# New spans for the parts of all head pairs in a scheduled kernel of attention and mixture-of-experts attention

## The chip, the cores and the metric

The kernel runs on one core of a Trainium2 chip. The metric is the device time of one launch, in microseconds (us). Three runs of the kernel before took 783.99, 787.72 and 788.71 us; the median is 787.72 us.

## The reference

Two layers of causal attention stand one behind the other. The first has 8 batches of 8 heads, 576 positions and 64 columns a head, and a learned decay; the second is a mixture of 4 experts, each an attention with one head of 64 columns over the 512 columns that the first layer gives, of which the two with the highest gate logits count at each position.

```python
# layer 1: q, k, v (8, 8, 576, 64), f (8, 8, 576)
scores = q @ k.T / 8
cum = cumsum(log(clip(f, 1e-4, 1)))
scores = where(causal, -1e9, scores + cum[:, :, :, None] - cum[:, :, None, :])
attn = exp(scores - max(scores)); attn /= sum(attn) + 1e-9
x = (attn @ v).transpose(0, 2, 1, 3).reshape(8, 576, 512)
# layer 2: w_gate (512, 4), wq, wk, wv (4, 512, 64), wo (4, 64, 512)
logits = x @ w_gate            # the two largest are kept, softmax over them is w
for e in range(4):
    q, k, v = x @ wq[e], x @ wk[e], x @ wv[e]
    a = causal_softmax(q @ k.T / 8)
    out += w_e * (a @ v @ wo[e])   # where e is one of the two experts
```

## The kernel before, in words

**Pairs.** The work is cut into 48 pairs of 64-row heads: in each batch four pairs of attention heads (kind "a", names such as a5_1 for batch 5, pair 1) and two pairs of experts (kind "m"). They follow each other in one list: the four "a" pairs of batch b, then the two "m" pairs of batch b-1. Two heads of 64 columns fill the 128 rows of TensorE (PE).

**Parts of a pair.** Every pair goes through the same parts, each a generator that emits its instructions in pieces.
- *prep*: an "a" pair transposes k and q (tp, L269), a "m" pair projects x by wk and wq (pp, L406, 12 matmuls to a half). Values are split into a high part, copied by ScalarE (ACT, L277 or L413), and the rest, subtracted by VectorE (DVE, L278 or L414). SyncE's DMAs move copies across partitions into the tiles kq and ka (L246).
- *vals* loads v. *front*, once per batch of experts, projects v and the gates (pv, L330; pg, L377), the gates on DVE.
- *max*: matmuls m0 to m3 (L432), masked maxima of them on DVE (L438, L449, L482), a transpose of the maxima (mp, L487), a negating copy on ACT (ms, L489), and a DMA (L246) that puts the negated maxima into one row of kq.
- *scores*: s0 (two), s1, s2 (two), s3 (two) in PSUM, each accumulated from a first half (L518), which needs prep alone, and a second half (L519), which also needs the row of negated maxima. ACT takes the exponential (L538 for s0, L548 for s1, L553 for s2, L565 and L569 for s3) into the tiles P and pl, GpSimd (POOL) clears what lies above the diagonal (L540, L504, L570) and adds up the parts (L576 to L579) into R.
- *attend*: P times v (oa and ob, L600, 4 and 10 matmuls), copied out to ot by ACT (L618, L626).
- For two pairs together, *sums*: column sums (sm, L643), their reciprocals on DVE (zt, L655 to L668) and a copy on ACT (rt, L669); then *apply*: for each of the two pairs two matmuls that spread the reciprocals over rows (cp, L686), two products on DVE (L687), a high part on ACT (L704) and a rest on DVE (L705), which form the input x of the experts (xh, xl) or of the output (yh, yl). For two expert pairs also *out*: the output projection (po, L727, 6 matmuls a block).

**Buffers.** PSUM has 2 buffers for m and mp (ps_m), 2 for s (ps_s), 1 for oa and ob (ps_o) and 3 for tp, pp, pv, pg, sm, cp and po (ps_x). A matmul into a buffer waits until the engine that empties it is done with what stood there.

**What sets the order.** Each part is given a span of places, two numbers in units of one pair, relative to its pair's position in the list: PLAN for each of the six pairs of a batch, HEAD with other numbers for the first nine pairs, TAIL for the last nine, W for the constants and the load of the weights. A part's pieces are spread evenly over its span by the weights that its generator yields, and all parts are merged by a heap:

```python
while heap:
    at, i = heapq.heappop(heap)
    x = tasks[i]
    ...
    w = next(x[7], None)           # emit the next piece of part i
    x[5] += w
    heapq.heappush(heap, (x[2] + (x[3] - x[2]) * x[5] / x[4], i))
```

The instructions emitted in that order are handed to the framework's scheduler (the tile context with its timeline simulation), which fixes the order of each engine's queue and where each semaphore is waited for. At run time an engine takes its queue strictly in that order. In the first three pairs dummy matmuls (warm) stand beside the prep.

## Time and profile before

| | before |
|---|---|
| median of 3 runs (lowest, highest) | 787.72 us (783.99, 788.71) |
| span of the profiled execution | 785.0 us |
| PE matmuls busy | 740.4 us (94%) |
| PE weight loads (PEld) busy | 594.7 us (76%) |
| DVE busy | 584.9 us (75%) |
| ACT busy | 469.5 us (60%) |
| POOL busy | 404.0 us (51%) |

Busy shares are averages over the whole span. Matmuls are pipelined and their ends are modelled, so that a busy PE may still be one that waits; weight loads (PEld) run beside the matmuls and show an idle time of their own in front of each. DVE's and ACT's busy times are sums of single instructions. PEclk is the clock granted to PE, as a share of full speed.

### The profile page before, as it was taken

What the parts mean: (1) busy time and instruction counts of PE and PEld (TensorE: products, weight loads), DVE (VectorE), ACT (ScalarE), POOL (GpSimd) and SP (SyncE); (2) the same over time, 40 slices, a digit from 0 to 9 for tenths busy, and PEclk for the clock granted to TensorE, in tenths of its full rate; (3) what the DMA queues carried; (4) which work ended last, traced back from release to release, by engine and by line L of the source; (5) the groups of instructions that cost most, each with busy time, mean ns of one, the idle gap of its engine ahead of it and who ended that gap; (6) DMA issues with size and microseconds to landing.
All of it is one profiled execution on the core that took longest, in us unless ns stands there. A gap on an engine that the chain in (4) does not pass through costs nothing.

```text
span 785.0 us, 16899 instructions
## 1 busy us (share of the span) xinstructions
PE 740.4 (94%) x5735; PEld 594.7 (76%) x5736; DVE 584.9 (75%) x1857; ACT 469.5 (60%) x1151; POOL 404.0 (51%) x770
## 2 busy tenths in 40 slices
...
GB/s 167 178 168 97 152 63 18 93 106 95 48 61 127 116 109 32 87 124 136 64 63 87 152 94 48 77 116 126 107 47 78 119 93 40 55 18 73 57 15 108
DMA packets 142234, 70.86 MB, mean 90 GB/s; under 512 B 124004, under 2 KB 124484, under 8 KB 142148
## 3 DMA queue, kind: packets, MB, share of 16 engines
...
## 4 chain that ended last, share of the span: by engine, by line
PE 74%; DVE 10%; ACT 6%; DMA 5%; issue 2%; SPq 2%; POOL 1%; POOLq 0%; DVEq 0%; ACTq 0%
PE pp_m L406 13%; PE ob_a L600 8%; PE pv L330 7%; PE po L727 7%; PE s_a L518 6%; PE m_a L432 6%; PE s_a L519 5%; PE tp_a L269 4%; PE s_m L519 3%; PE m_m L432 3%; PE s_m L518 3%; DMA kq<-ms_m 3%; PE sm_a L643 2%; DVE ka_a L278 2%; DMA kq<-ms_a 2%
## 5 line engine op out<-in xcount | busy, mean ns | idle before, releaser
L278 DVE TENSOR_TENSOR ka_a<-tp_a,kq 64x288 fp32r<-64x288 f32 x256 | 113.3, 451 | 18.8 <-ACT kq L277 8.5
L277 ACT ACTIVATE kq<-tp_a 64x288 fp32r<-64x288 f32 x256 | 100.2, 403 | 36.7 <-DVE ka_a L278 25.3
L438 DVE CUSTOM_DVE_ANT_0 junk_a<-m_a,mask 128x192 bf16<-128x192 f32 (+2 forms) x192 | 93.5, 487 | 37.0 <-PE m_a L432 29.8
L518 PE MATMUL s_a<-ka_a 128*128 128x320 f32 (+4 forms) x384 | 113.1, 314 | 2.6 <-ACT P_a L538 1.8
L432 PE MATMUL m_a<-kq 128*128 128x320 f32 (+4 forms) x384 | 102.0, 328 | 7.3 <-DVE mxs_a L438 5.5
L519 PE MATMUL s_a<-kq 128*128 128x320 f32 (+4 forms) x384 | 100.6, 297 | 2.2 <-DMA kq<-ms_a 2.2
L540 POOL TENSOR_SCALAR_AFFINE_SELECT P_a<-P_a 128x256 f32<-128x256 f32 x64 | 26.3, 415 | 135.8 <-ACT P_a L538 134.2
L414 DVE TENSOR_TENSOR ka_m<-pp_m,kq 64x288 fp32r<-64x288 f32 x128 | 58.2, 454 | 44.8 <-ACT kq L413 42.7
L413 ACT ACTIVATE kq<-pp_m 64x288 fp32r<-64x288 f32 x128 | 51.8, 404 | 62.4 <-PE pp_m L406 40.3
L504 POOL TENSOR_SCALAR_AFFINE_SELECT P_a<-P_a 128x128 f32<-128x128 f32 x128 | 37.6, 298 | 86.0 <-ACT P_a L553 84.6
L432 PEld LDWEIGHTS m_a<-kq 128*128 128x128 f32 (+1 forms) x384 | 63.8, 185 | 21.1 <-DVE mxs_a L438 11.8
L518 PEld LDWEIGHTS s_a<-ka_a 128*128 128x128 f32 (+1 forms) x384 | 69.5, 182 | 11.8 <-ACT P_a L538 2.5
L576 POOL TENSOR_TENSOR R_a<-P_a 128x448 f32<-128x448 f32 x64 | 73.5, 1148 | 3.9
L519 PEld LDWEIGHTS s_a<-kq 128*128 128x128 f32 (+1 forms) x384 | 68.8, 184 | 4.9 <-DMA kq<-ms_a 3.4
L600 PE MATMUL ob_a<-P_a,va 128*64 128x320 f32 (+1 forms) x512 | 69.2, 412 | 2.7 <-ACT ms_m L489 1.9
L518 PE MATMUL s_m<-ka_m 128*128 128x192 f32 (+3 forms) x192 | 57.6, 317 | 2.3 <-ACT P_m L548 1.0
L600 PEld LDWEIGHTS ob_a<-P_a,va 128*64 128x64 f32 x512 | 34.9, 137 | 31.0 <-POOL mxs_a L428 2.8
L438 DVE CUSTOM_DVE_ANT_0 junk_m<-m_m,mask 128x192 bf16<-128x192 f32 (+2 forms) x96 | 46.5, 485 | 14.8 <-PE m_m L432 12.9
L577 POOL TENSOR_TENSOR R_a<-R_a,P_a 128x320 f32<-128x320 f32 x64 | 55.2, 865 | 1.2
L519 PE MATMUL s_m<-kq 128*128 128x192 f32 (+2 forms) x192 | 50.6, 297 | 3.2 <-DMA kq<-ms_m 3.1
L432 PE MATMUL m_m<-kq 128*128 128x192 f32 (+2 forms) x192 | 48.4, 318 | 1.2 <-ACT ms_m L489 0.5
L504 POOL TENSOR_SCALAR_AFFINE_SELECT P_m<-P_m 128x128 f32<-128x128 f32 x64 | 18.6, 292 | 57.6 <-ACT P_m L553 51.4
...
## 6 DMA issues: line engine op xcount, KB each, us to landing
...
kq<-ex SPq DMA_DIRECT2D x94, 9.0 KB
...
```

The source lines that it names most:

```text
L277: made = nc.scalar.activation(hv, src, AF.Copy)
L278: nc.vector.tensor_tensor(lo[:, h, gs], src, hv.bitcast(F32), ALU.subtract)
L406: nc.tensor.matmul(pp[:, :HS], w[:, c, es], x[c][:, gs], start=(n == 0), stop=(n == 3 * KC - 1))
L414: nc.vector.tensor_tensor(lo[:, h, gs], src, hv.bitcast(F32), ALU.subtract)
L432: nc.tensor.matmul(dst, qB[0:K, h, i0 : i0 + dst.shape[0]], kB[0:K, h, j0:j1], start=True, stop=True)
L438: nc.vector.tensor_tensor_reduce(jk[:, :n], src, mask[:, MW - n :], 1.0, init, ALU.add, ALU.max, acc)
L504: return nc.gpsimd.affine_select(pv, pv, [[1, 128]], ALU.is_ge, 0.0, base=0, channel_multiplier=-1)
L518: nc.tensor.matmul(dst, kaf[:, c : c + m], qA[:, h, i0:i1], start=True, stop=False)
L519: nc.tensor.matmul(dst, kqf[0:K, c + h * S : c + h * S + m], qB[0:K, h, i0:i1], start=False, stop=True)
L576: g.tensor_tensor(r[:, h, 128:S], q[:, 320:768], q[:, 768:1216], ALU.add)
L577: g.tensor_tensor(r[:, h, 256:S], r[:, h, 256:S], q[:, 1216:1536], ALU.add)
L600: mm = nc.tensor.matmul(dst[64 * h : 64 * h + 64, c0 : c0 + rhs.shape[-1]], vs[h][0:kp, blk], rhs, start=first, stop=last,)
```

## The change

The code is the same; only the numbers of W, PLAN, HEAD and TAIL differ. Of the constants, the ends of two spans are later: the load of the weights, and the making of the constants.

```diff
...
-W = dict(d1=-1.9, l0=1.0, l1=4.0, c0=-1.7, c1=-1.3, x0=-0.9)
+W = dict(d1=-1.9, l0=1.0, l1=4.108, c0=-1.7, c1=-0.716, x0=-0.9)
...
```

In PLAN, a0's attend is about half a place earlier, a1's maxima start 0.18 later and its attend 0.4 earlier, a2's and a3's prep have other ends, m0's scores and the start of its attend are 0.2 to 0.4 earlier, m1's attend ends 0.37 earlier and its apply, for both expert pairs, stands 0.57 later; several others move by less than 0.1. In HEAD, vals of pair 1, attend of pairs 2, 5 and 6, prep of pairs 5, 6 and 7, scores of pairs 0, 5 and 7 and the first front have other numbers; in TAIL, out of the batch before the last three groups, and by small amounts attend, prep, scores and sums of the last three pairs.

Every instruction is still there once. Three places of the order on PE, in the repeating part of the program, show what moves. Rows are line, operation, tile written<-tiles read, shape.

First, PE around the last maxima of pair a5_1 (batch 5, pair 1): m3_a5_1 is the last maxima's matmul, mp_a5_1 the transpose that needs DVE to have reduced it. Before:

```order
L600 MATMUL oa_a5_0_6878<-P_a5_0_6532,va2_106 64x256 x2
L600 MATMUL oa_a5_0_6878<-P_a5_0_6532,va2_106 64x128 x2
L432 MATMUL m3_a5_1_6683<-kq1_112 128x320
L686 MATMUL cp_m3_0_6826<-rt_m3_0_6585,sel0_100 128x288
L686 MATMUL cp_m3_0_6829<-rt_m3_0_6585,sel0_100 128x288
L518 MATMUL s0_a5_1_6781<-ka_a5_1_6327 128x192
L487 MATMUL mp_a5_1_6687<-ident_93,mxs_a5_1_6644 10x128
```

The changed kernel, at the same mp:

```order
L432 MATMUL m3_a5_1_6695<-kq1_112 128x320
L600 MATMUL oa_a5_0_6778<-P_a5_0_6527,va2_106 64x256 x2
L600 MATMUL oa_a5_0_6778<-P_a5_0_6527,va2_106 64x128 x2
L518 MATMUL s0_a5_1_6744<-ka_a5_1_6365 128x192
L518 MATMUL s0_a5_1_6803<-ka_a5_1_6365 128x192
L269 MATMUL tp_a5_3_6874<-ident_93,qn_a5_3_6773 128x96 x3
L487 MATMUL mp_a5_1_6699<-ident_93,mxs_a5_1_6656 10x128
```

The four oa matmuls of pair a5_0 and the second s0 of a5_1, and three transposes of a5_3, now lie between m3 and mp, and the two cp of the expert pair m3_0 have left.

Second, PE at the two s2 of the second expert pair m4_1, whose two PSUM buffers are taken in turn: the second s2 goes into the buffer that s1 held. Before:

```order
L519 MATMUL s1_m4_1_7741<-kq1_112 128x256
L269 MATMUL tp_a6_1_7862<-ident_93,qn_a6_1_7692 128x96 x3
L518 MATMUL s2_m4_1_7757<-ka_m4_1_7274 128x448
L519 MATMUL s2_m4_1_7757<-kq1_112 128x448
L432 MATMUL m1_a6_0_7777<-kq2_113 128x256
L269 MATMUL tp_a6_2_7884<-ident_93,kn_a6_2_7878 128x96 x3
L518 MATMUL s2_m4_1_7821<-ka_m4_1_7274 128x448
L519 MATMUL s2_m4_1_7821<-kq1_112 128x448
```

The changed kernel:

```order
L518 MATMUL s2_m4_1_7759<-ka_m4_1_7271 128x448
L519 MATMUL s2_m4_1_7759<-kq1_112 128x448
L269 MATMUL tp_a6_1_7862<-ident_93,qn_a6_1_7730 128x96 x3
L432 MATMUL m1_a6_0_7779<-kq2_113 128x256
L727 MATMUL po3_2_7880<-oh_1059,yh_m3_0_0_6942 128x512
L727 MATMUL po3_2_7880<-ol_1060,yh_m3_0_0_6942 128x512
L727 MATMUL po3_2_7880<-oh_1059,yl_m3_0_0_6943 128x512
L727 MATMUL po3_2_7880<-oh_1059,yh_m3_0_1_6980 128x512
L727 MATMUL po3_2_7880<-ol_1060,yh_m3_0_1_6980 128x512
L727 MATMUL po3_2_7880<-oh_1059,yl_m3_0_1_6981 128x512
L432 MATMUL m2_a6_0_7790<-kq2_113 128x448
L518 MATMUL s2_m4_1_7831<-ka_m4_1_7271 128x448
```

One group of transposes has left, and an output block po of six matmuls and the maxima matmul m2_a6_0 now stand between s1 and the second s2, while the first s2 follows s1 with nothing in between.

Third, PE at the last two cp of the first expert pair (m4_0), whose products feed L687, L704 and L705. Before:

```order
L686 MATMUL cp_m4_0_8241<-rt_m4_0_7948,sel1_101 128x288
L519 MATMUL s0_a6_1_8154<-kq3_114 128x192
L518 MATMUL s0_a6_1_8154<-ka_a6_1_7690 128x320
L519 MATMUL s0_a6_1_8154<-kq3_114 128x320
L432 MATMUL m2_a6_2_8108<-kq0_111 128x448
L432 MATMUL m1_a6_2_8101<-kq0_111 128x256
L518 MATMUL s1_a6_1_8193<-ka_a6_1_7690 128x256
L519 MATMUL s1_a6_1_8193<-kq3_114 128x256
L518 MATMUL s1_a6_1_8193<-ka_a6_1_7690 128x256
L519 MATMUL s1_a6_1_8193<-kq3_114 128x256
L686 MATMUL cp_m4_0_8244<-rt_m4_0_7948,sel1_101 128x288
```

The changed kernel:

```order
L686 MATMUL cp_m4_0_8349<-rt_m4_0_7968,sel1_101 128x288
L518 MATMUL s3_a6_1_8338<-ka_a6_1_7728 128x320
L519 MATMUL s3_a6_1_8338<-kq3_114 128x320
L518 MATMUL s3_a6_1_8338<-ka_a6_1_7728 66x64
L519 MATMUL s3_a6_1_8338<-kq3_114 66x64
L518 MATMUL s3_a6_1_8338<-ka_a6_1_7728 66x64
L519 MATMUL s3_a6_1_8338<-kq3_114 66x64
L432 MATMUL m3_a6_2_8158<-kq0_111 128x320
L600 MATMUL oa_a6_1_8397<-P_a6_1_8115,va1_105 64x256 x2
L600 MATMUL oa_a6_1_8397<-P_a6_1_8115,va1_105 64x128 x2
L518 MATMUL s0_a6_2_8383<-ka_a6_2_7906 128x192
L686 MATMUL cp_m4_0_8352<-rt_m4_0_7968,sel1_101 128x288
```

The two cp stood among the second halves of s0 and s1 of pair a6_1, and stand now around its s3 and the oa of that pair.

## Rows read from the trace of the kernel before

**Rows 1.** stretch: length, busy PE, PEld, DVE, ACT, POOL (instructions), granted clock, DMA share, GB/s

```profile
40.00:105.00 65.00, 56.70 (x413) 42.36 (x414) 55.76 (x149) 43.07 (x106) 44.89 (x79) 0.95 0.61 128
145.00:188.00 43.00, 38.57 (x288) 27.66 (x288) 35.49 (x109) 27.58 (x69) 24.47 (x48) 0.96 0.47 106
188.00:679.00 491.00, 477.94 (x3871) 394.76 (x3871) 380.65 (x1251) 305.46 (x758) 254.80 (x487) 1.00 0.38 89
```

**Rows 2.** waits of weight loads, 188 to 679 us: total us, times, longest us

```profile
PEld s_m L519 <- DMA kq<-ms_m: 4.9, 9, 0.9
...
PEld s_a L519 <- DMA kq<-ms_a: 3.4, 5, 1.2
PEld mp_m L487 <- DVE mxs_m L438: 3.1, 5, 0.6
...
PEld mp_a L487 <- DVE mxs_a L438: 2.4, 5, 0.6
...
PEld s_m L518 <- ACT P_m L548: 2.0, 5, 0.4
...
PEld s_m L518 <- ACT pl L569: 1.3, 5, 0.3
PEld s_a L518 <- ACT P_m L565: 1.1, 5, 0.2
```

**Rows 3.** timeline 459.6 to 461.7 us: start, duration, engine, line, operation, out<-in, [idle before]

```profile
459.69 0.87 PE L600 MATMUL oa_a<-P_a,va 128*64 128x256 f32 x8
...
460.49 0.42 PE L432 MATMUL m_a<-kq 128*128 128x320 f32 x1
...
460.75 0.43 PE L686 MATMUL cp_m<-rt_m,sel 128*128 128x288 f32 x2
...
461.02 0.25 PE L518 MATMUL s_a<-ka_a 128*128 128x192 f32 x1
...
461.66 0.09 PEld L487 LDWEIGHTS mp_a<-ident,mxs_a 128*10 128x10 f32 x1 [0.59 <-DVE mxs_a L438]
```

**Rows 4.** chain of waits, 395 to 486.6 us: start, duration, what

```profile
435.48 2.59 DMA kq<-ms_m
...
445.79 1.42 PE po L727 x6
...
448.74 3.03 DMA kq<-ms_a
```

**Rows 5.** groups by line: busy us, mean ns, idle before by releaser

```profile
L413 ACT ACTIVATE kq<-pp_m 64x288 fp32r<-64x288 f32 x128 | 51.8, 404 | 62.4 <-PE pp_m L406 40.3 <-DVE ka_m L414 19.7
...
L538 ACT ACTIVATE P_m<-s_m 128x512 f32<-128x512 f32 x32 | 17.9, 595 | 8.8 <-PE s_m L519 8.6
```

**Rows 6.** timeline 496 to 502 us

```profile
498.00 1.57 SPq L246 DMA_DIRECT2D kq<-ms_a  x2
...
500.23 0.29 PE L406 MATMUL pp_m<-xh_a,qh 128*128 128x288 f32 x1
```

**Rows 7.** L705 and L665: ns min/median/max, first and last start us

```profile
L705 DVE TENSOR_TENSOR xl_a<-ot_a,xh_a x32: 744/757/4297, 73.8 to 707.5; 128x576 fp32r<-128x576 f32 x32
L705 DVE TENSOR_TENSOR yl_m<-ot_m,yh_m x16: 680/692/1430, 191.2 to 773.8; 128x512 fp32r<-128x512 f32 x16
...
L665 DVE TENSOR_TENSOR zt_a<-rc_a,zt_a x16: 174/228/3240, 63.5 to 701.4; 128x18 fp32r<-128x18 f32 x16
```

**Rows 8.** timeline of DVE and GpSimd at three places

```profile
63.48 3.24 DVE L665 TENSOR_TENSOR zt_a<-rc_a,zt_a 128x18 fp32r<-128x18 f32 x1
...
76.80 1.27 POOL L221 TENSOR_TENSOR ol<-st_o,oh 128x512 fp32r<-128x512 f32 x1
...
77.53 4.30 DVE L705 TENSOR_TENSOR xl_a<-ot_a,xh_a 128x576 fp32r<-128x576 f32 x1
...
463.55 0.95 DVE L705 TENSOR_TENSOR yl_m<-ot_m,yh_m 128x512 fp32r<-128x512 f32 x1
```

**Rows 9.** timeline of PE at 733 us

```profile
733.39 0.27 PE L487 MATMUL mp_m<-ident,mxs_m 128*10 128x128 f32 x1 [0.63 <-DVE mxs_m L482]
```

6 lines of the change are left out of this document (3 added, 3 removed).

## Prediction

> **What bounds the kernel now.** The first view to read is the table of stretches [rows 1]: busy time of each engine, the granted clock, and the DMA share. From 188 to 679 us, five and a half batches that repeat every 91 us, TensorE (PE) is busy for 477.94 of 491 us at a clock of 1.00, VectorE (DVE) for 380.65, and no other engine for more. From 40 to 105 us it is closer: DVE rises to 55.76 of 65 us and PE falls to 56.70, at a clock of 0.95; from 145 to 188 us DVE has 35.49 of 43 and the clock is 0.96. So the program fills its pipeline with DVE as a second bound beside PE, and then runs under PE alone. All instructions stay, so what the change can give is only the time in which PE waits, and what it can take is new waits.
>
> PE's busy time hides part of the waiting, because matmuls overlap. The second view is therefore the list of waits of PE's weight loads in the long stretch [rows 2]. Four kinds matter: the second half of the scores (L519) waits for the row of negated maxima, which comes by DMA (4.9 + 3.4 us); the transpose mp (L487) waits for the last maximum on DVE (3.1 + 2.4 us); the first half of the scores (L518) waits for ScalarE (ACT) to empty one of its two PSUM buffers (2.0 + 1.3 + 1.1 us). Together that is 16.2 us in 491, about 3 us a batch. Head and tail hold other waits, shown below.
>
> **The change, part by part.** Nothing is added or removed; the order on each engine moves.
>
> *mp behind the last maximum.* Before, mp of pair 1 stands behind the last m3 with two cp and one s0 between. The timeline [rows 3] shows m3 at 460.49, mp at 461.66, its weight load idle for 0.59 us. In the change four oa matmuls, a second s0 and three transposes stand there instead, as the order's rows show. The same oa block takes 460.49 - 459.69 = 0.80 us in the trace. The two cp that leave cost 461.02 - 460.75 = 0.27 us, so at least 0.5 us more lies in between, and with the transposes the 0.59 us are covered. Pair 1 of attention waits like this five times: -2.4 us, the whole row. Pair 1 of the experts (3.1 us, five times 0.6) gets one cp more, 0.14 us each: -0.7 us. Lower bound of this gain 0 (if DVE comes later by what was put between), upper 5.5.
>
> *Scores waiting for ACT.* The 2.0 us (s2's second half) stood behind two groups of three transposes and one m1; now a whole block po of six matmuls is among what stands there, 1.42 us in the chain of waits [rows 4], against a wait of 0.4: -2.0 us. The 1.1 us (s0 of the next batch behind L565) moves behind an oa block of 0.80 us: -1.1. The 1.3 us gets one cp: -0.7. Against this three places in a batch become short: s1 and the s3 halves of the same expert pair follow with only 0.8 to 0.9 us between the buffer's last matmul and its next first, where the exponential alone takes 0.60 us [rows 5]. If each waits 0.07 us, five batches pay +1.0; if 0.3, +4.5; if none, 0. Net -2.8.
>
> *The row by DMA.* From issue to the released matmul this takes 2.59 and 3.03 us [rows 4]. Pair 3 of attention loses cover: twelve pp matmuls that stood ahead of its first L519 now come behind three L519. Before, the DMA is issued at 498.00 and the pp block starts at 500.23 [rows 6]; so without the block PE arrives at 500.23 and the row at 498.00 + 2.59 to 3.03, a wait of 0.36 to 0.80 us. ACT now has one L413 (0.40 us [rows 5]) less ahead of the copy that feeds this DMA, which could take the wait back to 0. Five times 0.2 is +1.0, with 0 and +4.0 as ends; pair 0 gains 0.1 of cover each time, -0.5. Net +0.5.
>
> *DVE held up beside GpSimd.* The subtraction L705 of 576 columns takes 0.757 us as a rule and 4.297 at most, that of 512 columns 0.692; L665 takes 0.228 us as a rule and 3.240 at most [rows 7]. The timeline has the two long ones at 77.53 and 63.48 [rows 8], both while GpSimd ran tensor instructions back to back, the longest of them at 77.53 being one of 1.27 us. Both lie in the head, where DVE counts. In the long stretch the subtraction of the expert pair at 463.55 took 0.95 us beside the end of such a train. The change moves exactly this apply step: its last two cp stood among the s0 and s1 of a pair, and now stand around its s3, when GpSimd starts the train of sums (L576 to L579). Four subtractions a batch (L705 on 512 and 64 columns, for two pairs) then start beside a train. At 0.26 us each (0.95 less 0.69) that is 1.0 us of DVE a batch; DVE idles 22% of the stretch, and a quarter is taken to reach PE: +1.3 us. Bounds: 0, and the third rival below.
>
> *Head.* The first twelve transposes, maxima and scores hardly move. From there, six pp matmuls of batch 0 move ahead of the point where DVE has finished batch 0's last x, and a1's maxima move on DVE ahead of that point too: about 3.5 us more PE work, 2.9 us more DVE work, ahead of the same step. As DVE goes first there, the difference, 0.6 us, is a gain. In front of mp of pair 1 of batch 1 more work stands than before as well. Taken: -1.5. Bounds: -6.6, if both long held-up instructions come free ((3.24 - 0.23) + (4.30 - 0.76)), and +3, if one more is caught.
>
> *Tail.* mp of the last batch's pair 0 waits 0.63 us for DVE [rows 9]. The change puts a whole pv block of twelve matmuls ahead of it, and po and pp blocks ahead of the L519 of the pair before. The last scores lose such fillers. Net -0.6, ends -2 and +1.5.
>
> Sum: -3.1 - 2.8 + 0.5 + 1.3 - 1.5 - 0.6 = -6.2 us. The profiled execution spans 785.0 us; the three runs have 783.99, 787.72 and 788.71, so the median lies 2.7 us above the span, which I take as what lies around it and a run's scatter. 787.7 - 6.2 gives the forecast, **781.5 us**.
>
> Two rules of the Trainium skill bear on this. "Perfetto Trace Analysis", section "Identifying the Most-Contended Engine", says that matmul busy share is a poor measure of what TensorE has left, and weight-load busy the better one. By PE's own idle time, 491 - 477.94 = 13.1 us, the waits priced above are some 60% of what the weight loads show, and the sum would be about -4 instead of -6.2; the forecast goes by the weight loads. "SBUF — State Buffer", section "Who interferes with whom", says that a DVE instruction with two SBUF inputs and a GpSimd instruction that reads SBUF exclude each other for a whole instruction. The trace agrees that L705 is held, and at 77.53 it is held for longer (4.30 us) than any one instruction of GpSimd lasts there (1.27 us); by this rule the moved apply step costs up to one GpSimd instruction each time, which is the third rival.
>
> **The rivals.**
> - *Nothing in the long stretch.* DVE's order is tight enough that a maximum or a copy comes as much later as PE work was put ahead. For it: DVE is at 78% and its own queue holds the prep subtractions between the maxima. Against: those maxima stand at the same places of DVE's order, within an instruction. The first two terms (-5.9) go: **787 us**.
> - *The head comes free.* The two long holds of DVE in the head vanish because the trains of sums start at other times: -6.6 instead of -1.5, and neither the DMA term nor the apply term shows (-1.8): 781.5 - 5.1 - 1.8 = 774.6, **775 us**. For it: each of them needs a train without a gap, and these come in only two or three places. Against: L665 and the first L705 stay at nearly the same place relative to the scores of pairs 2 and 3.
> - *Slower: the apply step of the expert pair is held in the long stretch.* If two of its four subtractions a batch are held like those of the head (3.5 and 3.0 us), DVE loses 6.5 us a batch. With 20 us of idle DVE in 91, half would reach PE through the maxima queued behind: 3.25 x 5 = 16, in place of the 1.3, so 781.5 - 1.3 + 16 = **796 us**. It decides from 1.3 us of PE a batch on. Against: the same step at 463.55 already ran beside a train's end and lost 0.26.
>
> **How the numbers follow.** Forecast 0.42 (its own range 778 to 785), nothing in the long stretch 0.16, the head comes free 0.30, slower 0.12. About 1% is what a measurement of this kernel can tell from no change: faster means below 779.8 and slower above 795.6. Below lie the head's case (0.30) and the lower part of the forecast's range (0.12): 0.42. Slower: 0.12, and 0.02 for short places at their upper end with no gain elsewhere: 0.14. Same: 0.44. For 8 in 10 the range runs from 770 (the head's case, with mp and scores at full gain) to 791 (short places, the DMA row and half of the slower case at their ends).
>
> **What would show it.** In the profile after: the row "mp_a <- mxs_a" of the weight loads' waits gone, "mp_m <- mxs_m" at 2.4 rather than 3.1; "s_m <- P_m L548" at 0 for s2, small new ones for s1 and s3; "s_a <- DMA kq<-ms_a" up by 0 to 0.8 a batch, now in pair 3; L705's maximum and L665's in the head, and whether L705 of the expert pair is longer than 0.95 us in the long stretch. The forecast is wrong if the 91 us period does not fall by about 0.8 us, if DVE's busy time changes by more than 10 us, or if the head up to 188 us moves by more than 3 us.

## The result, and the profile after

| | before | after |
|---|---|---|
| median, the two run side by side (4 runs each) | 788.22 us | 763.52 us |
| lowest, highest | 783.99, 788.9 | 762.93, 764.07 |
| span of the profiled execution | 785.0 us | 762.4 us |

The ratio is 0.9704, with a 95% interval from 0.9678 to 0.973. The change makes the kernel 3.0% faster. The sign is that of the forecast. The size is not: 763.5 us lies 6.5 us below the range, whose lower end was 770.

The page's line of busy times, and the table of stretches (length, busy PE, PEld, DVE, ACT, POOL with instructions, granted clock, DMA share, GB/s) of the changed kernel:

```profile
PE 734.0 (96%) x5736; PEld 595.3 (78%) x5736; DVE 589.5 (77%) x1857; ACT 476.0 (62%) x1151; POOL 408.2 (54%) x770
40.00:105.00 65.00, 61.45 (x488) 47.38 (x488) 55.13 (x166) 46.77 (x116) 50.67 (x90) 1.00 0.63 132
178.00:653.40 475.40, 470.85 (x3856) 393.71 (x3855) 387.44 (x1246) 310.78 (x756) 253.68 (x482) 1.00 0.40 92
653.40:762.40 109.00, 97.71 (x692) 76.67 (x692) 59.66 (x174) 51.79 (x123) 41.81 (x76) 0.96 0.18 52
```

Read beside [rows 1], three things stand out. The same work of the long stretch takes 475 us instead of 491. The clock from 40 to 105 us is 1.00 instead of 0.95. In the tail it is 0.96, where nothing of the kind stood before (the profile before has 1.00 from 679 to 785 us).

Where the time went is told by one landmark, the start of the first oa matmul (L600) of a pair in the timeline. For pair 0 of batch 2 it moves from 186.43 to 176.52 us, for pair 2 of batch 7 from 678.09 to 652.46, and the end from 785.0 to 762.4. So the head gives 9.9 us, the long stretch (491.7 to 475.9 us) 15.7, and the tail takes back 3.0: together the 22.6 us by which the spans differ. (The medians differ by 24.7 us; each profile is of one execution.) The forecast had -1.5, -4.1 (-3.1, -2.8, +0.5 and +1.3) and -0.6.

The waits of weight loads in the long stretch, 178 to 653.4 us, of the changed kernel (total us, times, longest us):

```profile
PEld m_a L432 <- DVE gt L371: 2.8, 6, 0.5
...
PEld s_a L519 <- DMA kq<-ms_a: 1.8, 4, 0.6
PEld mp_m L487 <- DVE mxs_m L438: 1.6, 5, 0.3
...
PEld pg L377 <- DVE rr_a L668: 1.2, 4, 0.3
PEld pv L330 <- DVE lg L346: 1.2, 3, 0.4
PEld s_a L518 <- ACT kq L413: 1.0, 6, 0.2
...
PEld s_m L518 <- ACT pl L569: 0.9, 5, 0.2
...
PEld s_m L519 <- DMA kq<-ms_m: 0.4, 1, 0.4
```

Against [rows 2]: the waits for the row by DMA fall from 8.3 to 2.2 us, those of mp for DVE from 5.5 to 1.6, those of the scores for ACT from 4.4 (the three rows shown there) to 0.9, with a new 1.0 for ACT's L413. The waits of the gates and of the experts' value projection for DVE (pg, pv) grow, from 1.0 to 2.7 us with the small rows of the list. All rows of the list together fall from 47.9 to 33.4 us, by 14.5. That lies nearer to the 15.7 us than PE's own idle time, which falls from 13.1 to 475.4 - 470.85 = 4.6 us, by 8.5. The Trainium skill, "Perfetto Trace Analysis", section "Identifying the Most-Contended Engine", calls matmul busy time a poor measure and weight-load busy time the better one; here the trace agrees.

### The profile page after: what moved, and what is told of

Same layout as the page of the kernel before. It is cut to its first block, busy times and chain, and to the rows that moved or that the text cites. A ratio compares the mean times of both kernels' runs of the same rounds, so it can differ in the third digit from the quotient of the medians.

```text
span 762.4 us, 16940 instructions
## 1 busy us (share of the span) xinstructions
PE 734.0 (96%) x5736; PEld 595.3 (78%) x5736; DVE 589.5 (77%) x1857; ACT 476.0 (62%) x1151; POOL 408.2 (54%) x770
## 4 chain that ended last, share of the span: by engine, by line
PE 79%; DVE 7%; ACT 7%; DMA 3%; POOL 2%; issue 1%; SPq 0%; POOLq 0%; ACTq 0%; DVEq 0%
PE pp_m L406 13%; PE ob_a L600 8%; PE pv L330 7%; PE s_a L518 7%; PE s_a L519 6%; PE po L727 6%; PE m_a L432 5%; PE tp_a L269 4%; PE m_m L432 3%; PE ob_m L600 3%; PE oa_a L600 3%; PE s_m L518 2%; PE sm_a L643 2%; PE s_m L519 2%; ACT kq L277 2%; DMA kq<-ms_a 2%
## 5 line engine op out<-in xcount | busy, mean ns | idle before, releaser
L438 DVE CUSTOM_DVE_ANT_0 junk_a<-m_a,mask 128x192 bf16<-128x192 f32 (+2 forms) x192 | 93.3, 486 | 30.6 <-PE m_a L432 26.1
L518 PE MATMUL s_a<-ka_a 128*128 128x320 f32 (+4 forms) x384 | 112.3, 314 | 0.6 <-ACT P_a L538 0.6
L519 PE MATMUL s_a<-kq 128*128 128x320 f32 (+4 forms) x384 | 103.5, 300 | 1.1 <-DMA kq<-ms_a 1.0
L504 POOL TENSOR_SCALAR_AFFINE_SELECT P_a<-P_a 128x128 f32<-128x128 f32 x128 | 40.9, 325 | 97.2 <-ACT P_a L553 93.6
L540 POOL TENSOR_SCALAR_AFFINE_SELECT P_a<-P_a 128x256 f32<-128x256 f32 x64 | 26.0, 408 | 108.5 <-ACT P_a L538 107.2
L413 ACT ACTIVATE kq<-pp_m 64x288 fp32r<-64x288 f32 x128 | 51.9, 406 | 46.4 <-DVE ka_m L414 29.4
L518 PEld LDWEIGHTS s_a<-ka_a 128*128 128x128 f32 (+1 forms) x384 | 69.3, 183 | 7.1 <-ACT kq L413 1.4
L519 PEld LDWEIGHTS s_a<-kq 128*128 128x128 f32 (+1 forms) x384 | 69.5, 184 | 3.5 <-DMA kq<-ms_a 1.8
L600 PE MATMUL ob_a<-P_a,va 128*64 128x320 f32 (+1 forms) x512 | 69.2, 412 | 2.4 <-ACT ms_m L489 1.1
L438 DVE CUSTOM_DVE_ANT_0 junk_m<-m_m,mask 128x192 bf16<-128x192 f32 (+2 forms) x96 | 46.8, 487 | 19.4 <-PE m_m L432 15.4
L600 PEld LDWEIGHTS ob_a<-P_a,va 128*64 128x64 f32 x512 | 35.1, 136 | 30.5 <-POOL pl L570 2.8
L518 PE MATMUL s_m<-ka_m 128*128 128x256 f32 (+3 forms) x192 | 56.2, 310 | 0.8 <-ACT P_m L548 0.4
L519 PE MATMUL s_m<-kq 128*128 128x192 f32 (+2 forms) x192 | 49.5, 293 | 0.2 <-DMA kq<-ms_m 0.2
L330 PE MATMUL pv<-vh,xh_a 128*128 128x260 f32 x160 | 47.1, 294 | 0.9 <-DVE lg L346 0.9
```

The source lines that it names most:

```text
L330: nc.tensor.matmul(pv[:, :NV], l[c][:, t0 : t0 + 128], r[:, c], start=(n == 0), stop=(n == 3 * KC - 1))
L438: nc.vector.tensor_tensor_reduce(jk[:, :n], src, mask[:, MW - n :], 1.0, init, ALU.add, ALU.max, acc)
L518: nc.tensor.matmul(dst, kaf[:, c : c + m], qA[:, h, i0:i1], start=True, stop=False)
L519: nc.tensor.matmul(dst, kqf[0:K, c + h * S : c + h * S + m], qB[0:K, h, i0:i1], start=False, stop=True)
L600: mm = nc.tensor.matmul(dst[64 * h : 64 * h + 64, c0 : c0 + rhs.shape[-1]], vs[h][0:kp, blk], rhs, start=first, stop=last,)
```

## The experiments

Each changes one thing in the source, of the kernel before or of the changed one; the scheduler's order follows from it, and can change at other places too. The table sets all against the same landmark: where the head ends (first oa of batch 2, pair 0), how long the stretch from there to batch 7, pair 2 is, and the rest to the end of the span, from each profile. "Clock" is an estimate of the time lost in the head (40 to 190 us) because the granted clock stood at 0.50, that is 1.2 instead of 2.4 GHz: half of the length of those stretches. Each row is one profiled execution.

| kernel | head ends | stretch | rest | clock, head |
|---|---|---|---|---|
| before | 186.4 | 491.7 | 106.9 | 5.1 |
| after | 176.5 | 475.9 | 109.9 | 0.2 |
| e1_plan | 188.8 | 474.9 | 107.7 | 5.1 |
| e2_head | 175.7 | 490.1 | 106.9 | 0.2 |
| e3_tail | 188.8 | 491.4 | 110.8 | 7.3 |
| e4_apply_back | 176.3 | 491.9 | 113.2 | 1.7 |
| e5_a1prep | 188.8 | 486.9 | 106.3 | 8.5 |
| e6_head03 | 180.5 | 491.1 | 107.2 | 1.7 |
| e7_head48 | 179.6 | 490.0 | 106.9 | 1.7 |
| e8_onein | 180.3 | 491.5 | 106.8 | 1.7 |
| e9_oldtail | 176.5 | 475.7 | 109.1 | 0.0 |
| e10_kact | 184.1 | 498.3 | 110.1 | 4.8 |
| e11_a0prep | 176.5 | 476.1 | 108.9 | 1.3 |
| e12_row1 | 176.4 | 476.9 | 109.3 | 0.0 |
| e13_row2 | 176.1 | 479.3 | 109.5 | 0.0 |
| e14_twice | 190.1 | 491.9 | 106.9 | 6.8 |

How far one profile can be trusted is shown by e3, whose engines keep the order of the kernel before up to 675 us: its head ends 2.4 us later. The first 0.6 us of that stand there at the first oa of batch 0, pair 2 (63.09 and 63.71 us). Then the clock stands at 0.50 from 68.2 to 71.6 us, which it does not in the profile of before, and the first oa of pair 3 comes at 76.06 instead of 73.75 us, another 1.7 us later: half of those 3.4 us, as the estimate has it.

### Which table of spans brings what: e1_plan, e2_head, e3_tail

The kernel before, with the changed kernel's PLAN alone, with its HEAD and W alone, and with its TAIL alone.

```diff
-PLAN = {"a0": dict(prep=(-2.0, -1.2), vals=(0.15, -0.3), max=(-0.65, -0.6), scores=(-0.1, 0.7), attend=(1.3, 2.05)),
...
+PLAN = {"a0": dict(prep=(-2.0, -1.2), vals=(0.15, -0.3), max=(-0.65, -0.6), scores=(-0.086, 0.714), attend=(0.755, 1.505)),
...
```

> The kernel before with the new PLAN alone (HEAD, TAIL and W as before). Theory of stages: the time goes where a table's pairs run, so PLAN brings what the long stretch gained between the first oa of batch 2 and of batch 7 (455.9 us before, 442.3 in the changed kernel, -13.6), and little of the head: about 774.5 us, with a period of some 88.5 us. Rival, the gains hang together (the head's parts of batch 1 and the experts of batch 0 are partly PLAN's, and the clock falls or not by what stands there): 765 to 770 us, with the first oa of batch 2 some 5 us or more earlier than before.

Measured: 773.4 us beside 786.6, ratio 0.9841 (0.9817 to 0.9865). All of the gain lies in the long stretch, 16.8 us, and none in the head, which ends 2.4 us later in this profile and whose clock still loses 5.1 us.

```diff
-W = dict(d1=-1.9, l0=1.0, l1=4.0, c0=-1.7, c1=-1.3, x0=-0.9)
+W = dict(d1=-1.9, l0=1.0, l1=4.108, c0=-1.7, c1=-0.716, x0=-0.9)
...
-HEAD = {0: dict(prep=(-2.0, -1.2), vals=(1.0, 0.45), max=(-1.2, -0.75), scores=(0.0, 0.8), attend=(1.55, 2.05)),
...
+HEAD = {0: dict(prep=(-2.0, -1.2), vals=(1.0, 0.45), max=(-1.2, -0.75), scores=(0.047, 0.8), attend=(1.55, 2.05)),
...
```

> The kernel before with the new HEAD and W alone. Theory of stages: the head brings its whole -9.9 us (first oa of batch 2 at 176.5 instead of 186.4), the long stretch stays at 455.9: about 778 us, and the granted clock stays at 1.00 from 96 to 104 us. Rival, the head needs PLAN as well: less than half, 783 to 788 us, and a stretch at clock 0.50 remains near 97 to 103 us.

Measured: 774.31 us beside 786.6, ratio 0.9855 (0.9834 to 0.9876). The head ends 10.7 us earlier, at a clock of 1.00, and the stretch gains 1.6; about 778 was expected.

```diff
-TAIL = {-8: dict(out=(1.8, 2.55)),
...
+TAIL = {-8: dict(out=(1.015, 2.385)),
...
```

> The kernel before with the new TAIL alone. By what the changed kernel gives up between the first oa of batch 7 and the end (142.7 us before, 143.6 in the changed kernel), TAIL is worth about +0.9 us: 786.5 to 788.5. My prediction's step had -0.6. Rival, TAIL gains 2 us or more and the changed order of batch 7 hides it: under 785.5.

Measured: 788.7 us beside 785.92, ratio 1.0049 (1.0024 to 1.0073): slower. The rest is 3.8 us longer. DVE's one-input L369 on 128x5, 0.17 us in the kernel before, takes 2.98 us at 748.99 us, and the clock then stands at 0.50 from 750.9 to 757.8 us. (The profile is of one of the slower of ten launches, 792.68 us. Its head, with the old order, is 2.4 us later, as said above.)

The stretch's 16.8 and the head's 10.7 make the whole; the tail's new spans are a loss. Each of e1's stretch and e2's head is about 1 us beyond what the changed kernel has of it (15.7 and 9.9).

### What freed the row by DMA: e12_row1, e13_row2

The forecast gave the row's DMA a loss of 0.5 us; its waits gave back 6. The second expert pair of batch 3 shows why. Its mp, SyncE's queue (SPq) and the first L519 before, from the timeline (start, duration, engine, line, operation, [idle before]):

```profile
434.07 0.28 PE L487 MATMUL mp_m<-ident,mxs_m 128*10 128x128 f32 x1 [0.44 <-DVE mxs_m L438]
434.74 0.65 SPq L246 DMA_DIRECT2D ka_a<-kq  x1
438.11 0.19 PEld L519 LDWEIGHTS s_m<-kq 128*128 128x128 f32 x1 [0.55 <-DMA kq<-ms_m]
```

The row's DMA itself is the one issued at 435.48 in [rows 4]. The same place after:

```profile
416.31 0.28 PE L487 MATMUL mp_m<-ident,mxs_m 128*10 128x128 f32 x1
...
416.92 1.58 SPq L246 DMA_DIRECT2D kq<-ms_m  x2
...
420.02 0.25 PE L519 MATMUL s_m<-kq 128*128 128x192 f32 x1
```

Before, the copy ka_a<-kq of an attention pair's prep stands ahead of the row on SyncE and takes 0.65 us there, so the row is issued 435.48 - 434.07 = 1.41 us after mp. After, prep's new spans have moved that copy away, and the row is issued 0.61 us after mp. Three transposes have also come between mp and L519, whose matmul follows 3.71 us after mp without a wait. They are little cover: the weight load of L519 is ready 3.49 us after mp before (438.11 - 434.07, less its wait of 0.55), and 3.59 after. And the copy carries 288 KB, so that it fills the DMA engines too. To tell its place on the queue from the rest, the changed kernel got one (e12) or two (e13) further small DMAs (2.5 KB) on SyncE ahead of the row of every second expert pair; they only copy maxima to a tile that nothing reads.

```diff
+        if u["kind"] == "m" and u["p"] == 1: copy_bits(work.tile([5, 128], F32R, tag="dm", name="dm" + nm), ms[0:5])
```

> The changed kernel with one small DMA more on SyncE's queue ahead of the row of maxima of each second expert pair (eight in all; it copies 2.5 KB to a tile that nobody reads). The order of PE, ScalarE, DVE and GpSimd stays, save four matmuls near the end. Theory of SyncE's queue: the row is issued some 0.7 us later (1.3 instead of 0.6 us after mp, as in the kernel before), the spare 0.4 us there are used up, and a wait of 0.2 to 0.4 us a batch comes into the row s_m L519 <- DMA kq<-ms_m: 764.5 to 766. Rival, the place on the queue hardly matters since the transfer takes most of the 3 us: no wait there, 763 to 764.

```diff
+        if u["kind"] == "m" and u["p"] == 1: [copy_bits(work.tile([5, 128], F32R, tag=f"dm{i}", name=f"dm{i}" + nm), ms[0:5]) for i in range(2)]
```

> The same with two such DMAs ahead of each of these rows: issued some 1.5 us later than in the changed kernel. Theory of SyncE's queue: 0.9 to 1.2 us of wait at each of the eight rows, 4.5 to 6 us in the row s_m L519 <- DMA kq<-ms_m, and 767 to 771 in all. Rival, no more than 1 us in that row and under 765.

SyncE at that place, and the weight loads' wait from 178 to 655 us, in e12:

```profile
417.37 0.76 SPq L246 DMA_DIRECT2D dm_m<-ms_m  x1
418.17 1.49 SPq L246 DMA_DIRECT2D kq<-ms_m  x2
...
420.36 0.19 PEld L519 LDWEIGHTS s_m<-kq 128*128 128x128 f32 x1
...
PEld s_m L519 <- DMA kq<-ms_m: 1.3, 4, 0.4
```

The same in e13:

```profile
417.99 1.52 SPq L246 DMA_DIRECT2D dm_m<-ms_m  x2
419.55 1.43 SPq L246 DMA_DIRECT2D kq<-ms_m  x2
...
PEld s_m L519 <- DMA kq<-ms_m: 3.8, 12, 0.4
```

The third microsecond behind mp, first in the kernel before, then in e12, then in e10 of the next section (columns as above, the last two the DMA engines' share and GB/s; a packet counts where it starts, so that a share can pass 1):

```profile
436.07:437.07 1.00, 1.00 (x14) 0.77 (x11) 0.00 (x0) 0.21 (x1) 0.45 (x1) 1.00 0.94 214
```

```profile
418.76:419.76 1.00, 1.00 (x16) 0.77 (x12) 0.76 (x1) 0.16 (x2) 0.00 (x0) 1.00 0.02 5
```

```profile
437.40:438.40 1.00, 1.00 (x14) 0.77 (x11) 0.00 (x0) 0.15 (x1) 0.45 (x1) 1.00 1.02 258
```

The same place in all kernels that bear on it, those of later sections included, in us after the start of mp (second expert pair of batch 3):

| kernel | row issued | PE ready for L519 | its wait | DMA share, 2 to 3 us | 3 to 3.5 us |
|---|---|---|---|---|---|
| before | 1.41 | 3.49 | 0.55 | 0.94 | 0.65 |
| after | 0.61 | 3.59 | 0 | 0.02 | 0 |
| e12_row1 | 1.41 | 3.60 | 0 | 0.02 | 0 |
| e13_row2 | 2.17 | 3.65 | 0.27 | 0.02 | 0.01 |
| e5_a1prep | 1.22 | 3.67 | 0 | 0.13 | 0.02 |
| e10_kact | 1.38 | 3.53 | 0.91 | 1.02 | 0.43 |
| e11_a0prep | 1.48 | 3.52 | 0 | 0.88 | 0 |

Measured: e12 764.35 and e13 766.65 us beside 787.49, ratios 0.9707 (0.9693 to 0.9722) and 0.9737 (0.9723 to 0.9752). In e12 the row is issued 1.41 us after mp, as in the kernel before, PE is ready for it only 0.1 us later than there, and yet it does not wait. So neither the place on the queue nor the cover makes the wait of 0.55 us. (e12's theory of the queue asked for 0.2 to 0.4 us in each batch; its rival, for none.) Of the 0.9 us by which e12's row of waits grows, 0.35 stands at a second expert pair (batch 4), the rest at first ones; its time is not told apart from the changed kernel's (0.9707 beside 0.9704). In e13, issued at 2.17 us, the row waits at every second expert pair of the stretch, 3.3 us in all, and the stretch is 3.3 us longer: late enough on the queue, the place does cost time, but less than the 767 to 771 us that e13 was expected to take.

What is left is the copy's transfer. In the kernel before the DMA engines are full in the third microsecond (share 0.94; 0.83 to 0.99 in the five batches) and still at work after it (0.65), and the row releases L519 2.63 us after its issue; e13's row, with the engines idle, needs 1.75 us. At this place a row issued by 1.48 us waits where the engines work on beyond 3 us after mp, and nowhere else. e11, in which loads of v fill them up to that point, has no wait here, and 1.4 us in the five batches. No run puts the 288 KB back and moves nothing else, so this cause is what the others leave, not one that a run shows by itself.

### The same place from the kernel before: e5_a1prep, e10_kact

e5 moves a single span, the prep of pair 1 of attention, to its new place. e10 leaves the spans and has prep's copy issued on ACT's queue instead of SyncE's.

```diff
-"a1": dict(prep=(-2.0, -1.2), vals=(-0.25, 1.1),
+"a1": dict(prep=(-1.755, -1.228), vals=(-0.25, 1.1),
```

> The kernel before with one entry changed, a1's prep at (-1.755, -1.228). On SyncE's queue the copy ka_a<-kq of the next batch's pair 1 no longer stands ahead of the DMA that brings the row of maxima of the second expert pair, nor a copy ahead of pair 3's; PE's matmuls between mp and the first L519 of that expert pair hardly change (3.2 to 3.3 us). Theory of SyncE's queue: the wait of m1's first L519 (0.64 us a batch) goes though its cover is the same, the row s_m L519 <- DMA kq<-ms_m of the weight loads falls from 4.9 to under 1.5 us, time about 781 to 783 (with the longer way of mp of a1 in odd batches). Rival, only the matmuls in between count, as my prediction had it: that wait stays, the row stays over 3 us, and the time is 784.5 to 787.

Measured: 783.66 us beside 786.6, ratio 0.997 (0.9953 to 0.9987). The stretch gains 4.8 us: the row of the expert pairs no longer waits (4.9 to 0.3 us), nor does mp of the attention pairs for L438 (2.4 to 0). Three transposes came between mp and L519 here as well (ready at 3.67 us), and the row is still issued 1.22 us after mp, behind loads of v; what fell is the DMA engines' share, to 0.13. The order of PE changed from 150 us on, so that this run says more than its one entry. The head meanwhile ended 2.4 us later, with 3.4 us more lost to the clock, which took half of the gain back.

```diff
-                copy_bits(kA[0:64], kB[0:64])
+                nc.scalar.dma_start(kA[0:64].bitcast(F32), kB[0:64].bitcast(F32))
```

> The kernel before, in which the copy of the high part of k (ka<-kq after k's half of an attention pair's prep) is issued on ScalarE's queue instead of SyncE's; nothing else is written differently. For the second expert pair of batches 3 and 5 the PE work from mp to the first L519 stays 3.2 us. Theory of SyncE's queue: the DMA of the maxima's row is issued some 0.6 us after mp instead of 1.4, the row s_m L519 <- DMA kq<-ms_m falls from 4.9 to under 1.5 us; the time falls by up to 5 us (781 to 785), less what ScalarE loses by issuing. Rival, the copy and the row share the DMA engines and its transfer is what delays the row: the row of waits stays over 3.5 us, 786 or more.

ACT and SyncE at the second expert pair of batch 3 in e10 (mp starts at 435.40 us), from the timeline:

```profile
435.58 0.60 ACTq L283 DMA_DIRECT2D ka_a<-kq  x1
436.28 0.27 ACT L489 ACTIVATE ms_m<-mp_m 10x128 fp32r<-10x128 f32 x1 [0.73 <-PE m_a L432]
...
436.78 1.72 SPq L246 DMA_DIRECT2D kq<-ms_m  x2
```

Measured: 792.96 us beside 784.81, ratio 1.0109 (1.0085 to 1.0133): slower. The copy's issue now stands ahead of ms on ACT, and the row is issued 1.38 us after mp, as late as it was. The DMA engines are as full as before (1.02), and the row's waits stay at 4.5 us in the stretch: the rival that was named beforehand, that the copy's transfer delays the row (over 3.5 us, and 786 us or more), came true in both its numbers, and the theory of SyncE's queue (under 1.5 us) did not. The slower time is not priced by this place alone, since the scheduler laid out PE's work otherwise (at the second expert pairs of batches 2 and 4 the first L519 comes 6.8 us after mp instead of 4.1).

### The apply step put back: e4_apply_back

The changed kernel, with the apply step of the expert pairs at its old span, to see what DVE held up beside GpSimd costs in the long stretch.

```diff
-"m1": dict(prep=(-2.0, -1.2), max=(-0.9, -0.75), scores=(0.081, 0.667), attend=(1.109, 1.481), sums=(1.1, 0.2), apply=(2.766, 2.916), out=(5.097, 7.897))}
+"m1": dict(prep=(-2.0, -1.2), max=(-0.9, -0.75), scores=(0.081, 0.667), attend=(1.109, 1.481), sums=(1.1, 0.2), apply=(2.2, 2.35), out=(5.097, 7.897))}
```

> The changed kernel with m1's apply at its old span (2.2 to 2.35). Theory that the held subtractions reach PE (L705 +1.24 to 1.46 us and L664 +0.98 us in each batch beside GpSimd's sums): without them 1 to 2 us faster than the changed kernel, 761.5 to 762.5. Rival, DVE's lost time costs nothing in the long stretch and the later cp only changed what covers mp: in odd batches m3 to mp of pair 3 shrinks from 1.7 to 0.4 us of PE work and of m0 from 1.6 to 0.7, so new waits of some 0.5 us each, 764.5 to 767.

The weight loads' waits in e4, 178 to 655 us:

```profile
PEld s_m L519 <- DMA kq<-ms_m: 6.7, 11, 1.5
PEld mp_a L487 <- DVE mxs_a L438: 3.8, 6, 0.8
PEld s_a L519 <- DMA kq<-ms_a: 3.4, 4, 1.3
```

Measured: 782.44 us beside 786.6, ratio 0.9955 (0.9937 to 0.9972). Every expectation (761.5 to 767) missed. With one span put back the scheduler lays out the whole batch differently: the row's waits are back, mp's too, and the stretch is as long as in the kernel before (491.9). Of the 6.7 us, 5.4 stand at first expert pairs, where the row is issued 0.60 to 0.86 us after mp but PE is ready for it after 1.8 to 3.1. So this run says nothing clean on the apply step. It says that the gain belongs to the order that all spans give together: what one span is worth hangs on the others (e5's single span gained 4.8 us).

### What freed the head: e6_head03, e7_head48, e8_onein

The head holds two things: DVE instructions held up beside GpSimd, and a clock that falls. Summed over instructions that took over 0.4 us longer than the median of their line, tiles and shape, the holds are 10.6 us in the kernel before (40 to 188 us) and 3.0 after (to 178). e6 takes W and pairs 0 to 3 of the new HEAD, e7 pairs 4 to 8. e8 keeps the old spans, but gives L665 and L705 of the first sums and apply step one SBUF input instead of two; it thereby leaves out the subtraction of the low parts of those pairs.

```diff
-1: dict(prep=(-2.0, -1.2), vals=(0.1, 0.45),
...
+1: dict(prep=(-2.0, -1.2), vals=(0.66, 1.249),
...
```

> The kernel before with the new W and the new HEAD of pairs 0 to 3 alone. Theory that the two long holds of DVE (L665 for 3.24 us at 63, L705 for 4.30 us at 78, both in the sums and the apply step of pairs 0 and 1) and the fall of the clock behind them are the head's loss: their entries are here, so this run has neither hold, keeps clock 1.00 from 97 to 103 us and takes most of the -12.3 us of HEAD and W: 776 to 779. Rival, what counts is where the maxima, prep and first front of pairs 4 to 8 stand on DVE at 80 to 170 us: 784 to 788.

```diff
-6: dict(prep=(-2.9, -1.25), vals=(0.05, 0.45), max=(-1.0, -1.55), scores=(0.55, 0.85), attend=(0.9, 1.65)),
...
+6: dict(prep=(-2.452, -1.25), vals=(0.05, 0.45), max=(-1.0, -1.55), scores=(0.55, 0.85), attend=(1.426, 2.176)),
...
```

> The kernel before with the new HEAD of pairs 4 to 8 alone. Theory of the holds: L665 and L705 are still held for 3 us and more, the clock still falls near 97 us, 783 to 787. Rival, the order of pairs 4 to 8 brings the head's gain: 775 to 780, with both holds still there.

```diff
-                nc.vector.tensor_tensor(l, x, h.bitcast(F32), ALU.subtract)
+                nc.vector.tensor_scalar(l, x, 0.0, None, ALU.mult) if nm == "_a0_0" else nc.vector.tensor_tensor(l, x, h.bitcast(F32), ALU.subtract)
```

> The kernel before, in which L665 of the first sums and the two L705 of the first apply step (batch 0, pairs 0 and 1) read one tensor from SBUF instead of two (a product with 0 in place of the difference, so the low parts of the reciprocals and of two x tiles are left out); their POOL neighbours stay, and the order of PE, DVE and POOL moves only locally around 75 to 110 us. Theory that DVE is held because both it and GpSimd read two tensors: L665 takes under 0.3 us and L705 under 0.8 us, DVE is 6.6 us earlier, the clock stays 1.00 at 97 to 103 us, and the first oa of batch 1's pair 1 comes 6 to 10 us earlier: 778 to 781. Rival, the hold does not depend on the number of inputs: the long instructions stay within 0.5 us, 785 to 789. Second rival, the holds go but DVE was waiting anyway: 784 to 787.

The timeline of DVE in e7, then in e8, the same instructions as the first and third line of [rows 8]:

```profile
63.05 3.24 DVE L665 TENSOR_TENSOR zt_a<-rc_a,zt_a 128x18 fp32r<-128x18 f32 x1
...
77.47 0.76 DVE L705 TENSOR_TENSOR xl_a<-ot_a,xh_a 128x576 fp32r<-128x576 f32 x1
```

```profile
62.04 0.28 DVE L665 TENSOR_SCALAR zt_a<-rc_a 128x18 fp32r<-128x18 f32 x1
69.42 1.32 DVE L705 TENSOR_SCALAR xl_a<-ot_a 128x576 fp32r<-128x576 f32 x1
74.66 1.89 DVE L705 TENSOR_SCALAR xl_a<-ot_a 128x576 fp32r<-128x576 f32 x1
```

Measured, beside 785.92 us: e6 780.47, ratio 0.9937 (0.9915 to 0.9959); e7 778.1, 0.9903 (0.9875 to 0.9931); e8 780.53, 0.994 (0.9919 to 0.996). The head ends 5.9, 6.9 and 6.1 us earlier. In e6 L665 takes 1.15 us and the long L705 2.31; in e7 L665 keeps its 3.24 us, and L705 alone comes free; in e8 L665 is free, L705 half. In all three the clock loses 1.7 us instead of 5.1. So L665 alone is not the cause, and the parts do not add up: 5.9 + 6.9 is more than e2's 10.7. What the three share is a shorter L705 and 3.4 us less lost to the clock, which is about half of what each gains. By the sum used above the holds are 6.6, 8.8 and 4.9 us (e2: 5.5), and the gains do not follow them: e7, with the least taken away, gains most. Its own theory (783 to 787 us) missed, and its rival, that the order of pairs 4 to 8 brings the gain (775 to 780), met the time; e6, expected between 776 and 779, came out 1.5 us above. Nor does e8 show the holds alone, though its time was met: the scheduler's order of PE and DVE between 50 and 130 us changed with it, and its L665 ended at 62.32 us, before GpSimd's sums began at 62.76. So e2 shows that the head's spans bring the gain, and how much of it is the holds stays open.

The clock's part is steadier. The six profiles with the old head (before, e1, e3, e5, e10, e14) lose 4.8 to 8.5 us to it, the seven with the new one (after, e2, e4, e9, e11, e12, e13) 0 to 1.7; by the price that e3 shows, that is some 3 to 8 us of the gain.

### What the clock does: e14_twice

The kernel before, with all maxima matmuls of three pairs issued twice in the head, so that PE has more to do.

```diff
-            nc.tensor.matmul(
+            for _ in range(2 if nm in ("_a1_1", "_a1_2", "_m0_1") else 1): nc.tensor.matmul(
```

> The kernel before, in which the matmuls of the maxima of pairs 1 and 2 of batch 1 and of the second expert pair of batch 0 are each done twice (same result), so that PE has about 1.3 us more to do in each of the three places where it waits for DVE ahead of a fall of the clock; the order around them moves a little. Theory that the clock falls because PE waits there, and that its fall costs half of the time at 0.50 (10.2 us, so 5.1): with more work PE keeps 1.00 at one or both places, 781 to 785 in spite of the 4 us of added work. Rival, the fall does not follow from the waiting: clock as before, 786 to 790.

First the kernel before, by stretches of the head (columns as above: length, busy PE, PEld, DVE, ACT, POOL, granted clock, DMA share, GB/s):

```profile
90.00:96.50 6.50, 4.26 (x34) 2.87 (x33) 5.52 (x19) 2.87 (x7) 2.60 (x6) 1.00 0.81 178
97.00:103.00 6.00, 5.93 (x26) 5.65 (x27) 4.27 (x14) 3.26 (x6) 0.81 (x2) 0.50 0.03 6
154.00:161.00 7.00, 4.42 (x33) 3.31 (x31) 6.83 (x19) 4.74 (x14) 5.83 (x10) 1.00 0.54 124
161.00:164.50 3.50, 3.50 (x17) 1.64 (x17) 2.15 (x6) 0.66 (x2) 1.09 (x3) 0.56 0.33 74
```

The changed kernel, in its head and in its tail:

```profile
90.00:96.50 6.50, 5.72 (x42) 5.32 (x42) 6.44 (x20) 5.51 (x12) 2.00 (x4) 1.00 0.62 135
...
716.00:723.00 7.00, 3.19 (x25) 2.19 (x23) 6.80 (x18) 2.39 (x8) 6.51 (x12) 1.00 0.00 1
723.00:729.50 6.50, 6.18 (x56) 3.83 (x57) 2.15 (x7) 1.21 (x3) 0.23 (x1) 0.51 0.01 3
```

And e14, at the first of its three falls:

```profile
76.00:83.00 7.00, 5.54 (x43) 3.95 (x43) 6.84 (x8) 4.31 (x11) 6.76 (x9) 1.00 0.57 124
83.00:87.00 4.00, 3.88 (x14) 3.28 (x15) 3.81 (x14) 3.52 (x9) 1.84 (x3) 0.60 0.67 138
```

Last e8, whose wait at 150 us is that of the kernel before at 154 us:

```profile
150.00:157.00 7.00, 4.42 (x33) 3.08 (x33) 6.81 (x17) 4.74 (x14) 6.09 (x12) 1.00 0.59 137
157.00:165.00 8.00, 7.49 (x57) 5.83 (x53) 7.26 (x23) 5.28 (x13) 1.88 (x5) 1.00 0.48 106
```

Measured: 791.21 us beside 787.49, ratio 1.0057 (1.0035 to 1.0079), above the ranges of both theories. In the kernel before, each fall to 0.50 stands behind a stretch in which PE waited (busy for 4.26 of 6.5 and 4.42 of 7 us); the changed kernel has 5.72 of 6.5 in the first of these places and no fall, and in its tail 3.19 of 7 us and then a fall. In e14 the clock falls three times, once behind a stretch with 5.54 of 7 us busy and twice within stretches with 3.55 and 2.97 of 5, and loses 6.8 us. More matmuls did not keep the clock up. PE waited ahead of each of these falls, but a wait does not bring one each time: e8 has the same 4.42 of 7 us at 150 us and keeps 1.00 behind it, and e3 has a fall at 68.2 us where the profile of before, with the same order and the same wait (5.21 and 5.22 of 7 us busy ahead of 68 and 67.5 us), has none. So a missing fall in one profile, as in e6 to e8, may be chance, and what decides it stays open.

### The tail and one more span: e9_oldtail, e11_a0prep

e9 is the changed kernel with the old TAIL; e11 is e9 with another prep of pair 0.

```diff
-TAIL = {-8: dict(out=(1.015, 2.385)),
...
+TAIL = {-8: dict(out=(1.8, 2.55)),
...
```

> The changed kernel with the old TAIL. In the changed kernel L369 of the last gate, 0.1 us of work, takes 2.9 us at 719.75 beside GpSimd's sums, pg waits 4.2 us for the gate at 719, and the clock stands at 0.50 from 723 to 729.5; with the new TAIL alone the same hold and the fall are there at 749 to 757, with PLAN alone neither. Theory that this hold is TAIL's: without it 757 to 760.5, L369 under 0.5 us, no fall of the clock before the last output blocks. Rival, the tail follows from PLAN's order of batch 7: 763 to 765, and pg still waits.

DVE's L369 in the changed kernel, and GpSimd beside it, from the timeline; then the wait of a weight load in its tail:

```profile
719.75 2.98 DVE L369 TENSOR_SCALAR sm<-sm 128x5 f32<-128x5 f32 x1
...
719.94 1.67 POOL L577 TENSOR_TENSOR R_m<-R_m,P_m 128x320 f32<-128x320 f32 x2
721.57 1.14 POOL L578 TENSOR_TENSOR R_m<-R_m,P_m 128x192 f32<-128x192 f32 x2
722.78 0.45 POOL L579 TENSOR_TENSOR R_m<-R_m,pl 64x128 f32<-64x128 f32 x1
...
PEld pg L377 <- DVE gt L371: 4.2, 1, 4.2
```

Measured: 762.18 us beside 784.81, ratio 0.9726 (0.9689 to 0.9764), against 0.9704 for the changed kernel: the same within what is measured, where 757 to 760.5 us were expected. L369 is back at 0.17 us and pg's wait of 4.2 us is gone, but the clock still falls (1.7 us lost instead of 3.4), and other waits of about 1 us stand there instead. The rest is 109.1 us, 2.2 longer than in the kernel before with the same TAIL: the order of the tail hangs on what PLAN leaves ahead of it.

```diff
-PLAN = {"a0": dict(prep=(-2.0, -1.2), vals=(0.15, -0.3),
+PLAN = {"a0": dict(prep=(-1.9, -1.1), vals=(0.15, -0.3),
...
```

> The changed kernel with the old TAIL and a0's prep 0.1 later (-1.9 to -1.1). It puts a group of transposes between the last maximum and mp of the second expert pair (0.6 us of PE work there becomes 1.5 us), and leaves the other places of the long stretch as they are. Theory that a wait goes by the work between: mp_m <- mxs_m of the weight loads falls from 1.6 us to about 0, five times 0.2 us of PE, so 1 us faster than the changed kernel with the old TAIL, 756 to 760. Rival, what is put ahead of mp delays DVE's maxima by as much: the wait stays and the time is the same or longer than that kernel's.

Measured: 761.74 us beside 784.81, ratio 0.9712 (0.969 to 0.9734): no different from e9, where 756 to 760 us were expected. The last wait of mp for DVE (1.6 us) is gone, and the expert pairs' row waits 2.0 instead of 0.4 us, as much.

## Why the prediction was wrong, step by step

**mp behind the last maximum: right, too small.** Forecast -3.1 us, with the row of attention gone and that of the experts at 2.4. The first is gone, with a further 0.8 us of mp waiting for L482 that the list of before also had; the second is 1.6. That is about -4.7.

**Scores waiting for ACT: right.** Forecast -2.8. The row behind L548 is gone, that behind L565 too, the third is 0.9, and the new wait is 1.0 (for L413). With the smaller rows of the list the waits of L518 for ACT fall from 5.6 to 2.8 us. The short places that were priced at 1.0 do not show among the waits; that the wait for L413 has the same size, and the net so comes out, is luck.

**The row by DMA: the step that failed in the long stretch.** Forecast +0.5, found -6.1 (8.3 to 2.2). The step took the 2.59 to 3.03 us from issue to release as fixed, asked how much PE work stands between at one pair (pair 3 of attention), and took the issue to stay where it was, but for one L413 of ACT. What changed is the time from issue to release: 2.63 us at the second expert pair of batch 3 before, 2.2 at most in e12, 1.75 in e13, with the 288 KB copy gone from ahead of the row and the DMA engines' share in the third microsecond after mp at 0.02 instead of 0.94. The second expert pairs give 3.2 of the 6.1 us, the first ones 1.3, attention's pair 0 gives 1.6, though its row is now issued 1.24 us after mp instead of 0.60 (batch 5). The wait that was forecast at pair 3 does not show. That the copy left its place stood in the order before the run; the step did not look at what else the DMA engines had to carry, nor at the expert pairs, whose row was the largest of [rows 2]. The cause is what e12 and e13 leave, as said there.

**DVE beside GpSimd: the mechanism right, DVE's loss too small, the net near by luck.** Forecast +1.3, from 1.0 us of DVE a batch. In the long stretch the groups read (count | busy us, mean ns | idle before), first before, then after:

```profile
L705 DVE TENSOR_TENSOR yl_m<-ot_m,yh_m 128x512 fp32r<-128x512 f32 x12 | 9.0, 754 | 1.4 <-ACT yh_m L704 1.0
...
L664 DVE CAST zt_m<-rc_m 128x18 fp32r<-128x18 f32 x5 | 1.3, 264 | 0.0
```

```profile
L705 DVE TENSOR_TENSOR yl_m<-ot_m,yh_m 128x512 fp32r<-128x512 f32 x12 | 16.4, 1368 | 2.2 <-ACT yh_m L704 2.2
...
L664 DVE CAST zt_m<-rc_m 128x18 fp32r<-128x18 f32 x5 | 5.8, 1156 | 0.2
```

The expert pairs' L705 takes 0.61 us more on the mean, not 0.26, and the cast L664 ahead of their reciprocals 0.89 more. With the 64-column L705 (3.4 to 4.7 us) that is 13.2 us of DVE in the stretch, about 2.5 a batch. (In e4, with the apply step at its old span, the median of this L705 is back at 0.69 us, that of L664 stays at 1.14.) What shows of it in pv and pg is 1.7 us of PE in the whole stretch, an eighth of DVE's loss and not a quarter: two errors that cancel. The slower rival asked for 6.5 us of DVE a batch and for 1.3 us of PE a batch; DVE was held for two fifths of the first, and the rival falls.

**Head: the step that failed most.** Forecast -1.5 with -6.6 as its lower end, found -9.9 (e2: -10.7). The bound counted the two long holds, which did shrink (L665 from 3.24 to 1.15 us, L705 from 4.30 to 0.99):

```profile
L665 DVE TENSOR_TENSOR zt_a<-rc_a,zt_a x16: 179/200/1150, 62.3 to 674.1; 128x18 fp32r<-128x18 f32 x16
```

It never priced the clock, although [rows 1] has 0.95 and 0.96 in the two stretches that were read. That is 5.1 us lost before and 0.2 after. What the holds by themselves gave is not shown: e6 to e8 do not separate them from the order and the clock. "The head comes free" was the rival nearest to the truth. That its 775 us is what e2 measured (774.31) is chance: it added the gains of mp and the scores, which e2 does not have.

**Tail: wrong sign.** Forecast -0.6, with +1.5 as the end; found +3.0. The mp wait of [rows 9] was weighed, but not a DVE instruction that comes to stand beside GpSimd's sums, and a clock that falls behind the wait (3.4 us).

**The range.** Its lower end combined the free head with the full gain of mp and scores. It kept the DMA term between +4 and -0.5 and the head above -6.6, and both bounds were one-sided for the same reason: each took the one place that had been looked at for all of them. "Nothing in the long stretch" falls by e1. Two of the prediction's own signs of being wrong came: the head moved by 9.9 us and not under 3, and the period (first oa of batch 2 to that of batch 7, a fifth) fell from 91.2 to 88.5 us, by 2.7 and not 0.8. The third did not: DVE's busy time rose by 4.6 us, under 10.

The long stretch, summed: mp, the scores and the row give 4.7 + 2.8 + 6.1 = 13.6 us; pv and pg take back 1.7 (1.0 to 2.7, with the small rows of the list); transposes tp that wait for nothing but their own queue give 2.3 (4.6 to 2.3). That makes 14.2 of 15.7 us. The rest of the list moves both ways, with m_a behind DVE's L371 (2.8 us) now the largest row; all rows together give the 14.5 us named above, and the last 1.2 were not traced.
